# Attention with block summaries and an MLP on one core: summary scores of 128 queries, a spread on another engine, and a new order

## The chip, the cores and the metric

The kernel runs on one core of one Trainium2 chip. The metric is the device time of one launch in microseconds (us). Each launch is also seen by a profiler in one execution, whose span (first to last instruction) is somewhat shorter than its device time.

## What is computed

Inputs are q, k and v of shape (4, 8, 768, 64) in float32 (batch, heads, positions, channels) and the two weight matrices of an MLP, 512 x 2048 and 2048 x 512. Cut to what matters:

```
k_sum = k.reshape(B, H, 24, 32, D).max(axis=3)          # one summary key per 32 positions
v_sum = v.reshape(B, H, 24, 32, D).mean(axis=3)         # one summary value
scores_l = scale * q @ k^T, -1e9 where |i - j| >= 16    # near keys
scores_s = scale * q @ k_sum^T + log(32)                # 24 summary keys
a = softmax([scores_l, scores_s]) ;  x = a @ [v, v_sum] # (3072 tokens, 512)
h = x @ w_in ;  g = h * erf(softplus(h)) ;  out = g @ w_out
```

Of the near scores only those within 15 positions count, so a stretch of 64 queries needs a window of 96 keys, and with the 24 summaries 120 columns.

## The kernel before

The 3072 tokens are worked off in six chunks of 512. A **quad** is one chunk of one pair of heads (128 channels): 24 quads, four to a chunk. For a quad there are: the scores (`scores`, L479: near keys and summaries of eight blocks of 64 queries and two heads, into two banks of 4 x 120 columns), the softmax (`softmax`, L517: maximum on VectorE L535, exponential on ScalarE L541, reciprocal L553 on VectorE, normalization on VectorE L557 or ScalarE L560), eight transposes (`transp`, L571) and a copy on ScalarE (L575, tile `ptr`), the product with the values (`av`, L596, tile `px`) and a split of the result into a high and a low part (`xsplit`: `xh` is a cast on either engine, `xl` a subtraction on VectorE, L612). The MLP then runs in periods of four blocks of 128 columns: the first product (`mm1`, L635, tile `h`; each product is three matmuls, high by high, high by low and low by high), the activation, and the second product (`mm2`, L696 and L700, tile `ops`). Four quads make the 512 input channels of a chunk; so a chunk's first product needs all four quads, and quad p gives the p-th of its four parts.

Weights come as raw words (`rw`, loaded at L308, 1024 KB each) and are put together by VectorE in three steps (L325, L328, L331), then split into a high part (cast on ScalarE, L275) and a low part (VectorE, L347).

The first four quads have no earlier work to hide behind and take a way of their own. Their keys (`kf`, L420, 384 KB each), queries (`qf`, L421, 256 KB), the values of the sequence (`vt`, L425, two halves of 768 KB) and the windows of the values (`vwf`, L428, 384 KB) are loaded directly. VectorE reduces the summary keys (L431). TensorE sums the values into summaries (L437, six matmuls, tile `vs`), ScalarE copies them to `vsum` (L440), and they are spread into the last 24 rows of each quad's `vwf`: the first quad's by GpSimd (L443), the others' by a DMA each (L445, 96 KB). The scores are three steps: mask (L491, L492), near keys and summaries (both L500).

All that is written as operations with a duration for each engine that may do them, and `Plan.order` puts them in a row by list scheduling: the operation that can start first on an engine goes next; among those ready at that time, the one with the least key. The key is a due time (for TensorE the operation's number) plus an offset from the table `TUNE`, which has entries for the operations (1262 entries before, 1841 now). `FILL` puts matmuls with zeros ahead of chosen TensorE operations (`busy`, L738, tile `idle`); 14 more stand at the very start. Loads are issued by SP, in the planned order, on one queue.

The operations of the first quads that the change touches, as they are before:

```
on({"POOL": 1.1}, lambda e: e.tensor_copy(st[0]["vw"][LW:NK], vsum[LW:NK, 0:1, :].to_broadcast([NS, NB, 128])), ["vsum00"], ["vwg0"])
pe(0.5, lambda: keys(lambda r, j: [(LW, ksum[r, 0, qd])]), [f"qf{qd}", f"ksum0{qd}"], banks)
```

Of the kernel before, what the change touches and what calls it, by code (L numbers as in the profile page):

```python
# [26 lines left out]
NB = T // 64  # L27
NI = NB // 2
NT = T // 128
NS = 24  # L30
LW = 96
NK = LW + NS
# [12 lines left out]
FILL = {20: 7, 40: 8, 41: 9, 61: 6, 93: 14, 111: 6}  # L45
# [139 lines left out]
def block_attention_mlp(ctx: ExitStack, tc: tile.TileContext, q_t, k_nat, k_win, v_tok, v_nat, v_win, w_in, w_out, out):  # L185
    nc = tc.nc
# [7 lines left out]
    def sb(shape, dtype, name, tag=None):  # L194

        n = math.prod(shape[1:])
        if n % 128 == 0:
            return pool.tile(shape, dtype, name=name, tag=tag or name)
        t = pool.tile([128, -(-n // 128) * 128], dtype, name=name, tag=tag or name)[0:shape[0], 0:n]
        return t if len(shape) == 2 else t.rearrange("p (a b) -> p a b", a=shape[1]) if len(shape) == 3 else t.rearrange("p (a b c) -> p a b c", a=shape[1], b=shape[2])  # L200

    def ps(name, tag):
        return psum.tile([128, 2, 512] if tag == "pa" else [128, 512], F32, name=name, tag=tag)
# [48 lines left out]
    ksum = sb([128, 2, NP, NS], F32, "ksum")  # L252
    vrows = [slice(LW, NK), slice(0, NS)]
    vsum = sb([NK, NP, 128], F32, "vsum")
# [7 lines left out]
    def pe(us, fn, r=(), w=(), **kw):  # L262
        return P.add({"PE": us}, lambda e: fn(), r, w, **kw)

    def on(us, fn, r=(), w=(), **kw):
        return P.add(us, lambda e: fn(engines[e]), r, w, **kw)

    def act(us, fn, r=(), w=(), **kw):
        return P.add({"ACT": us}, lambda e: fn(), r, w, **kw)

    def dma(kb, fn, r=(), w=(), hold=2.0, **kw):
        return P.add({"SP": max(0.45, kb / 350.0)}, lambda e: fn(), r, w, hold=hold, **kw)
# [78 lines left out]
    def parts(m, n):  # L351
        u = ("o", m // 2, m % 2)
        split(u, n, f"a{m}", lambda: w32[u])
# [54 lines left out]
    st = {}  # L408
# [24 lines left out]
    def vsum_first(bank):  # L433
        def go(t):
            if t == 0:
                tiles[bank] = ps("vs", bank)
            nc.tensor.matmul(tiles[bank][0:NK], lhsT=pick[:, 20 - 4 * t:140 - 4 * t], rhs=vts[t // 3][:, t % 3], start=(t == 0), stop=(t == 5))  # L437
        for t in range(6):
            pe(0.87, lambda t=t: go(t), [f"vt{t // 3}"], [bank])
        act(0.5, lambda: nc.scalar.copy(vsum[LW:NK], tiles[bank][LW:NK].rearrange("s (p c) -> s p c", p=NP)), [bank], [f"vsum0{p}" for p in range(NP)])  # L440
        for p in range(NP):
            if p == 0:
                on({"POOL": 1.1}, lambda e: e.tensor_copy(st[0]["vw"][LW:NK], vsum[LW:NK, 0:1, :].to_broadcast([NS, NB, 128])), ["vsum00"], ["vwg0"])  # L443
            else:
                dma(100, lambda p=p: nc.sync.dma_start(out=st[p]["vw"][LW:NK], in_=vsum[LW:NK, p:p + 1, :].to_broadcast([NS, NB, 128])), [f"vsum0{p}"], [f"vwg{p}"])  # L445
# [33 lines left out]
    def scores(qd, banks=("pa",)):  # L479

        s = st[qd]

        def mask():
            for n in banks:
                tiles[n] = ps(n, n)
            s["sc"] = [tiles["pa"][:, 0], tiles["pa"][:, 1]] if banks == ("pa",) else [tiles[n] for n in banks]
            s["both"] = tiles["pa"] if banks == ("pa",) else None
            m0 = mask_at[qd // NP % 3]
            for sc in s["sc"] if qd < MQ else []:

                nc.tensor.matmul(sc[:, 0:NI * NK], lhsT=ident_h, rhs=mask_h[:, m0:m0 + NI], start=True, stop=False, skip_group_check=True)  # L491
                nc.tensor.matmul(sc[:, 0:NI * NK].rearrange("q (i c) -> q i c", i=NI)[:, :, LW:NK], lhsT=ones, rhs=cst.rearrange("o (i c) -> o i c", i=NI), start=False, stop=False, skip_group_check=True)  # L492

        def keys(parts):
            for j in range(NB):
                for a in range(2):
                    r, o = slice(64 * a, 64 * a + 64), slice(64 * (j % 2), 64 * (j % 2) + 64)
                    for n, rhs in parts(r, j):
                        n += j // 2 * NK
                        nc.tensor.matmul(s["sc"][a][o, n:n + rhs.shape[-1]], lhsT=s["qb"][r, 64 * j:64 * j + 64], rhs=rhs, start=qd >= MQ, stop=True, skip_group_check=True)  # L500

        def near(r, j):

            kn, k0 = kfirst[qd], 64 * j - 16
            return [(0, kn[r, k0:k0 + LW])] if j else [(0, kn[r, 0:16]), (16, kn[r, 0:LW - 16])]

        def both():
            mask()
            keys(lambda r, j: [(0, s["kw"][r, j])])
        if qd >= NP:  # L510
            pe(1.06 if qd >= MQ else 1.64, both, ["qb", "kw"] + (["mh"] if qd < MQ else []), banks)
        else:
            pe(0.58, mask, ["mh"], banks)
            pe(0.96, lambda: keys(near), [f"qf{qd}", f"kf{qd}"], banks)
            pe(0.5, lambda: keys(lambda r, j: [(LW, ksum[r, 0, qd])]), [f"qf{qd}", f"ksum0{qd}"], banks)
# [216 lines left out]
    banks = [("pa",), ("h0", "h1"), ("o0", "o1"), ("h0", "h1")]  # L732
    idle = ps("idle", "o3")

    def busy(n):

        for _ in range(n):
            nc.tensor.matmul(idle[:, 0:256], lhsT=zeros[:, 0:128], rhs=zeros, start=True, stop=True)  # L738
# [10 lines left out]
    for p in range(3):  # L749
        ksum_first(p)  # L750
        scores(p, banks[p])
        softmax(p, banks[p])
    vsum_first("o2")
    ksum_first(3)
    scores(3, banks[3])
    softmax(3, banks[3])
    convert(units[0])
# [31 lines left out]
    def attend(n):  # L789

        scores(n)
        softmax(n)
        load_quad_v(n)
# [95 lines left out]
    free = {"PE": 4.15, "DVE": 1.4, "ACT": 4.2, "POOL": 5.2, "SP": 0.7}  # L889
    plan = P.order(free, lambda n: 60 if n < 330 else 0, TUNE, "exp")  # L890
    sets = {"exp": "exp_and_others", "log": "natural_log_exp_and_others", "sig": "sigmoid_and_others"}
    filling = True
    for o in plan:
        if o["on"] == "PE":
            filling = filling and "o3" not in o["w"]
            if filling:
                busy(FILL.get(o["n"], 0))
        if "load" in o:
# [42 lines left out]
```

## Time and profile before

| | |
|---|---|
| runs | 636.8, 637.97, 638.75 us, median 637.97 |
| profiled execution | 638.24 us, span 635.3 us |
| TensorE busy | 629.0 us |
| ScalarE busy | 431.7 us |
| VectorE busy | 392.0 us |
| GpSimd busy | 19.6 us |
| moved by the DMA queues | 89.30 MB |

How it is read: busy time is the time in which an engine works on instructions; weight loads of TensorE (PEld) lie beside its matmuls. A chain of waits is followed back from the last instruction to what released each step. A table by stretches gives busy times and the busy share of the DMA engines between two times from the start of the span. A timeline lists an engine's instructions with start and duration, several of one kind in one row; instructions of a row overlap, so the duration of a row can reach past the start of the next.

### The profile page before, as it was taken

The numbers are of one execution on the slowest core, as the hardware profiler recorded it, in microseconds if no ns is written. First come the engines' busy times: TensorE is split into PE (matmuls) and PEld (weight loads), VectorE is DVE, ScalarE is ACT, GpSimd is POOL, SyncE is SP. The second block draws the span as 40 slices with busy tenths as digits, with TensorE's granted clock in tenths as the row PEclk, the third lists the DMA queues.
The fourth block names the chain that finished last, engine by engine and source line by source line (L and its number), as shares of the span: only waits on it lengthen the run. The fifth ranks groups of instructions, "written<-read, shape, count | busy, mean of one in ns | idle before, by whom it ended". The sixth has DMA issues, their size and how long they took to land.

```text
span 635.3 us, 10484 instructions
## 1 busy us (share of the span) xinstructions
PE 629.0 (99%) x4264; PEld 502.0 (79%) x4264; DVE 392.0 (62%) x502; ACT 431.7 (68%) x742; POOL 19.6 (3%) x56
## 2 busy tenths in 40 slices
PE   8999999999999999999999999999999999999997
PEld 6776557888888887888888888888888888888886
DVE  4999999756766647676655645735555454334442
ACT  5669977978949648976484684674954952863470
POOL 2001010100000000000000000000000000000000
PEclk9999999999999999999999999999999999999999
DMA  9998947724641334653152640224451103140013
GB/s 320 259 375 299 349 160 243 263 83 164 213 131 48 104 98 158 237 153 104 51 164 82 206 143 1 79 71 142 145 180 32 32 1 132 67 133 0 2 63 135
DMA packets 28483, 89.30 MB, mean 141 GB/s; under 512 B 3028, under 2 KB 8468, under 8 KB 23316
## 3 DMA queue, kind: packets, MB, share of 16 engines
q1 hardware_dynamic: 27860, 88.13, 41.9%
q8 instruction: 33, 0.54, 0.4%
q10 hardware_dynamic: 576, 0.52, 0.2%
q14 instruction: 14, 0.11, 0.1%
HBM read 75.89 MB, written 10.49 MB: 136 GB/s over the span
## 4 chain that ended last, share of the span: by engine, by line
PE 96%; DMA 2%; SPq 0%; ACT 0%; issue 0%; DVE 0%; ACTq 0%
PE h L635 41%; PE ops L700 38%; PE ops L696 4%; PE px L596 4%; PE pa L500 3%; PE pa L571 3%; DMA rw<-w_in 1%; PE vs L437 1%; DMA qf<-q_t 1%; PE idle L738 1%; PE vt L395 0%; SPq L445 0%; PE pa L491 0%; PE o L500 0%; PE h L500 0%
## 5 line engine op out<-in xcount | busy, mean ns | idle before, releaser
L635 PE MATMUL h<-xh,w 128*128 128x512 f32 x768 | 253.4, 396 | 0.0
L700 PE MATMUL ops<-w,gh 128*128 128x512 f32 x704 | 227.9, 393 | 0.0
L635 PEld LDWEIGHTS h<-xh,w 128*128 128x128 f32 x768 | 144.2, 188 | 32.1 <-issue 1.6
L700 PEld LDWEIGHTS ops<-w,gh 128*128 128x128 f32 x704 | 132.4, 188 | 28.4 <-issue 0.6
L635 PE MATMUL h<-xl,w 128*128 128x512 f32 x384 | 149.5, 389 | 0.0
L650 ACT ACTIVATE wt<-hc 128x1024 f32<-128x1024 f32 x48 | 50.7, 1057 | 136.5 <-DVE hc L275 136.4
L700 PE MATMUL ops<-w,gl 128*128 128x512 f32 x352 | 137.1, 390 | 0.0
L899 ACT ACT_TABLE_LOAD x105 | 134.7, 1283 | 1.9
L275 DVE COPY hc<-h 128x512 f32<-128x512 f32 x81 | 55.7, 690 | 124.0 <-PE h L635 123.4
L635 PEld LDWEIGHTS h<-xl,w 128*128 128x128 f32 x384 | 72.2, 188 | 15.1 <-issue 1.0
L700 PEld LDWEIGHTS ops<-w,gl 128*128 128x128 f32 x352 | 66.1, 188 | 13.0
L676 DVE TENSOR_TENSOR hc<-wt,hc 128x1024 f32<-128x1024 f32 x44 | 52.9, 1221 | 19.1 <-ACT wt L664 19.1
L659 ACT ACTIVATE wt<-wt,stats 128x1024 f32<-128x1024 f32 x48 | 55.4, 1153 | 0.6
L683 DVE TENSOR_TENSOR gl<-hc,gh 128x1024 fp32r<-128x1024 f32 x44 | 52.9, 1221 | 0.6
L541 ACT ACTIVATE pr<-pr,stats 128x120 f32<-128x120 f32 x128 | 48.7, 382 | 5.5 <-DVE stats L550 5.4
L664 ACT ACTIVATE wt<-wt 128x1024 f32<-128x1024 f32 x48 | 49.8, 1058 | 0.4
L275 DVE CAST gh<-hc 128x1024 fp32r<-128x1024 f32 x44 | 30.0, 692 | 28.0 <-PE ops L700 27.1
L575 ACT COPY ptr<-pa 120x1024 f32<-120x1024 f32 x24 | 24.2, 1009 | 12.0 <-PE px L596 6.5
L696 PE MATMUL ops<-a32s,gw 128*128 128x512 f32 x64 | 29.2, 595 | 0.0
L463 POOL COPY kw<-ksum 128x96 f32<-128x96 f32 (+1 forms) x28 | 14.8, 544 | 440.4 <-DMA kw<-k_win 440.4
L525 DVE TENSOR_TENSOR pr<-pa,mask_sb 128x960 f32<-128x960 f32 x16 | 18.5, 1157 | 10.3 <-PE pa L500 10.3
L596 PEld LDWEIGHTS px<-ptr,vw 120*64 120x64 f32 x640 | 20.3, 138 | 5.3 <-DVE hc L275 1.6
(110 smaller groups left out, 499.1 us busy)
## 6 DMA issues: line engine op xcount, KB each, us to landing
w<-dr SPq DMA_DIRECT2D x20, 1024.0 KB
kw<-k_win SPq DMA_DIRECT2D x20, 480.0 KB
rw<-w_in SPq DMA_DIRECT2D x8, 1024.0 KB
rw<-w_out SPq DMA_DIRECT2D x8, 1024.0 KB
vw<-v_win SPq DMA_DIRECT2D x20, 384.0 KB
qb<-q_t SPq DMA_DIRECT2D x20, 256.0 KB
rows<-k_nat SPq DMA_DIRECT2D x12, 384.0 KB
rows<-v_nat SPq DMA_DIRECT2D x12, 384.0 KB
```

The source lines that it names most:

```text
L275: e.copy(o, i) if e is nc.scalar else e.tensor_copy(o, i)
L541: nc.scalar.activation(s["pr"][:, j], s["pr"][:, j] if qd >= MQ else s["sc"][j // NI][:, i * NK:(i + 1) * NK], AF.Exp, scale=0.125, bias=s ...
L596: nc.tensor.matmul(xo[r, o], lhsT=s["vw"][:, j, r], rhs=s["pt"][:, a, o], start=True, stop=True)
L635: nc.tensor.matmul(hs[k, f][:, 0:T], lhsT=w[m], rhs=xt[ch, cc][x], start=(cc == 0 and n == 0), stop=(cc == 3 and n == 2))
L650: nc.scalar.activation(wt[k, s], hc[k, s], AF.Tanh, scale=0.5)
L659: act(1.06, lambda n=n: nc.scalar.activation(wt[k, n], wt[k, n], AF.Ln, scale=-0.49999994, bias=half_b), [s], [s], table=("log",))
L664: act(0.96, lambda n=n: nc.scalar.activation(wt[k, n], wt[k, n], AF.Erf, scale=-1.0), [s], [s], table=("sig",), after=after)
L676: e.tensor_tensor(hc[k, n], wt.pop((k, n)), hc[k, n], op=ALU.mult)
L683: e.tensor_tensor(gs[k, n][1], hc.pop((k, n)), f32(gs[k, n][0]), op=ALU.subtract)
L696: nc.tensor.matmul(os_[ch, t], lhsT=x[0][:, i % 2, t * 128:(t + 1) * 128], rhs=w32["o", g, i // 2][:, i % 2], start=first, stop=last)
L700: nc.tensor.matmul(os_[ch, t], lhsT=x[y][:, i % 2, t * 128:(t + 1) * 128], rhs=w[m], start=first and n == 0, stop=last and n == 2)
L899: nc.scalar.preload_act_table_set(sets[o["load"]])
```

## The change

Three parts. The summary scores of the first four quads are made for 128 queries and one head at a time, 8 matmuls a quad instead of 16 of 64 queries (a product of float32 runs as two records). The first quad's summary rows are spread by ScalarE instead of GpSimd. And both tables, `TUNE` and `FILL`, are new, so that the order on all engines, the first transfers' on SP among them, is another one. `FILL` has 57 matmuls with zeros instead of 50. From the new function on, line numbers are 7 higher.

```diff
-TUNE = {0: (-833.887, 1.5, 0, None), ...}
-FILL = {20: 7, 40: 8, 41: 9, 61: 6, 93: 14, 111: 6}
...
+FILL = {48: 5, 30: 9, 31: 4, 51: 7, 60: 8, 61: 4, 81: 5, 92: 15}
@@ vsum_first
             if p == 0:
-                on({"POOL": 1.1}, lambda e: e.tensor_copy(st[0]["vw"][LW:NK], vsum[LW:NK, 0:1, :].to_broadcast([NS, NB, 128])), ["vsum00"], ["vwg0"])
+                act(0.95, lambda: nc.scalar.copy(st[0]["vw"][LW:NK], vsum[LW:NK, 0:1, :].to_broadcast([NS, NB, 128])), ["vsum00"], ["vwg0"])
@@ scores
+        def summary():
+
+            for i in range(NI):
+                for a in range(2):
+                    r = slice(64 * a, 64 * a + 64)
+                    nc.tensor.matmul(s["sc"][a][:, i * NK + LW:i * NK + NK], lhsT=s["qb"][r, 128 * i:128 * i + 128], rhs=ksum[r, 0, qd], start=False, stop=True, skip_group_check=True)
+
...
-            pe(0.5, lambda: keys(lambda r, j: [(LW, ksum[r, 0, qd])]), [f"qf{qd}", f"ksum0{qd}"], banks)
+            pe(0.27, summary, [f"qf{qd}", f"ksum0{qd}"], banks)
```

The first place is SP's row of transfers between the first values and the fourth `vwf`. Before:

```order
L425 DMA vt<-v_tok 128x3x512 x2
L308 DMA rw<-w_in 128x2048
L428 DMA vwf<-v_win 96x1024
L421 DMA qf<-q_t 128x512
L428 DMA vwf<-v_win 96x1024
L308 DMA rw<-w_in 128x2048
L445 DMA vwf<-vsum 24x8x128 x2
L308 DMA rw<-w_in 128x2048
L428 DMA vwf<-v_win 96x1024
L445 DMA vwf<-vsum 24x8x128
L428 DMA vwf<-v_win 96x1024
```

And now, from the start on:

```order
L421 DMA qf<-q_t 128x512 x2
L420 DMA kf<-k_nat 128x768
L425 DMA vt<-v_tok 128x3x512
L420 DMA kf<-k_nat 128x768 x3
L421 DMA qf<-q_t 128x512
L425 DMA vt<-v_tok 128x3x512
L308 DMA rw<-w_in 128x2048
L428 DMA vwf<-v_win 96x1024
L421 DMA qf<-q_t 128x512
L428 DMA vwf<-v_win 96x1024
L308 DMA rw<-w_in 128x2048
L445 DMA vwf<-vsum 24x8x128 x3
```

Behind these stand a `w_in`, two `vwf` and a `w_in` now. Ahead of both pieces stand or stood the first keys and queries, of which two `kf` came first before and two `qf` and a `kf` now; the three transfers of `vsum` stand together, so the third is now ahead of the third `w_in` and the third `vwf`.

The second place is TensorE from the third quad's product with its values (`px`) to the end of the fourth's. Before:

```order
L596 MATMUL px<-ptr,vwf 64x64 x16
L635 MATMUL h<-xh,w 128x512
L635 MATMUL h<-xl,w 128x512
L635 MATMUL h<-xh,w 128x512
L571 MATMUL pa<-ident,prf 120x128 x8
...
L635 MATMUL h<-xh,w 128x512
L596 MATMUL px<-ptr,vwf 64x64 x16
L635 MATMUL h<-xh,w 128x512
L635 MATMUL h<-xl,w 128x512
...
L738 MATMUL idle<-zeros 128x256
```

And now:

```order
L603 MATMUL px<-ptr,vwf 64x64 x16
L578 MATMUL pa<-ident,prf 120x128 x8
L642 MATMUL h<-xh,w 128x512
L642 MATMUL h<-xl,w 128x512
...
L642 MATMUL h<-xh,w 128x512
L603 MATMUL px<-ptr,vwf 64x64 x16
L642 MATMUL h<-xh,w 128x512
L642 MATMUL h<-xl,w 128x512
```

The fourth quad's transposes (`pa`) stood three matmuls of the first product behind the third `px` and nine ahead of the fourth; they now stand directly behind the third `px`, with nine between them and the fourth. The six matmuls with zeros behind the fourth are gone. Ahead of the third `px`, the same happened to the third transposes: they stood ahead of the second `px`, with 18 matmuls of the first product between it and the third, and stand behind it now, with three such matmuls ahead of the second `px` and 15 between.

The third place is VectorE from the first quad's split on. Before:

```order
L275 CAST xh<-px 128x512
L550 TENSOR_SCALAR stats<-stats 128x8
L612 TENSOR_TENSOR xl<-px,xh 128x512
L325 TENSOR_SCALAR a_489<-rw 128x1024
L328 SCALAR_TENSOR_TENSOR a_489<-rw,a_489 128x1024
L331 SCALAR_TENSOR_TENSOR a_489<-rw,a_489 128x1024
L612 TENSOR_TENSOR xl<-px,xh 128x512
L545 TENSOR_SCALAR stats<-stats 128x8
L325 TENSOR_SCALAR a_538<-rw 128x1024
L553 RECIPROCAL stats<-stats 128x8
L328 SCALAR_TENSOR_TENSOR a_538<-rw,a_538 128x1024
L347 TENSOR_TENSOR w<-a_489,w 128x1024
```

And now:

```order
L557 TENSOR_SCALAR stats<-stats 128x8
L619 TENSOR_TENSOR xl<-px,xh 128x512
L325 TENSOR_SCALAR a_439<-rw 128x1024
L328 SCALAR_TENSOR_TENSOR a_439<-rw,a_439 128x1024
L331 SCALAR_TENSOR_TENSOR a_439<-rw,a_439 128x1024
L552 TENSOR_SCALAR stats<-stats 128x8
L560 RECIPROCAL stats<-stats 128x8
L619 TENSOR_TENSOR xl<-px,xh 128x512
L325 TENSOR_SCALAR a_526<-rw 128x1024
L328 SCALAR_TENSOR_TENSOR a_526<-rw,a_526 128x1024
L331 SCALAR_TENSOR_TENSOR a_526<-rw,a_526 128x1024
L347 TENSOR_TENSOR w<-a_439,w 128x1024
```

The cast `xh` of the first quad went to ScalarE; the fourth quad's reciprocal went ahead of the second `xl` and of the third weight's first step (L325); the second weight's last step (L347) went behind the third weight's first three.

## Rows read from the trace of the kernel before

**Rows 1.** The page: busy time of each engine, and the chain by engine.

```profile
PE 629.0 (99%) x4264; PEld 502.0 (79%) x4264; DVE 392.0 (62%) x502; ACT 431.7 (68%) x742; POOL 19.6 (3%) x56
...
PE 96%; DMA 2%; SPq 0%; ACT 0%; issue 0%; DVE 0%; ACTq 0%
```

**Rows 2.** The table by stretches: busy us of each engine, clock, DMA share, GB/s.

```profile
core 0: us, PE busy (x) PEld busy (x) DVE busy (x) ACT busy (x) POOL busy (x), PEclk, DMA share, GB/s
6.90:16.20 9.30, 8.55 (x234) 6.80 (x235) 6.04 (x13) 5.59 (x32) 0.00 (x0) 1.00 1.05 396
16.20:34.10 17.90, 17.53 (x207) 12.84 (x206) 16.73 (x25) 12.62 (x43) 1.11 (x1) 1.00 1.00 259
42.20:80.00 37.80, 37.80 (x196) 23.84 (x194) 37.35 (x44) 36.21 (x54) 1.81 (x2) 1.00 0.92 336
34.10:631.70 597.60, 597.60 (x3800) 479.18 (x3800) 366.64 (x460) 409.80 (x664) 14.80 (x28) 1.00 0.40 132
```

**Rows 3.** Groups by line: busy us, mean ns of one, idle before.

```profile
L738 PE MATMUL idle<-zeros 128*128 128x256 bf16 x64 | 9.7, 305 | 1.1 <-DVE zeros L210 1.1
...
L500 PE MATMUL h<-ksum,qf 64*64 64x24 f32 x64 | 1.3, 210 | 0.0
L443 POOL COPY vwf<-vsum 24x1024 f32<-24x1024 f32 x1 | 1.1, 1107 | 15.8 <-ACT vsum L440 15.8
```

**Rows 4.** Timeline of SP: start us, duration us, transfers that it issues.

```profile
9.10 0.33 SPq L308 DMA_DIRECT2D rw<-w_in  x1
21.34 1.82 SPq L445 DMA_DIRECT2D vwf<-vsum  x2
...
23.79 0.43 SPq L428 DMA_DIRECT2D vwf<-v_win  x1
```

**Rows 5.** Timeline of TensorE, 7 to 43 us.

```profile
7.68 0.67 PE L500 MATMUL h<-ksum,qf 64*64 64x24 f32 x32
8.28 0.94 PE L738 MATMUL idle<-zeros 128*128 128x256 bf16 x7
...
28.32 1.15 PE L596 MATMUL px<-ptr,vwf 120*64 120x64 f32 x32
...
34.07 1.15 PE L596 MATMUL px<-ptr,vwf 120*64 120x64 f32 x32 [0.27 <-ACT prf L560]
...
35.97 1.04 PE L571 MATMUL pa<-ident,prf 128*120 128x128 f32 x8
36.76 0.47 PE L635 MATMUL h<-xh,w 128*128 128x512 f32 x1
...
38.69 0.40 PE L635 MATMUL h<-xh,w 128*128 128x512 f32 x1
39.02 1.15 PE L596 MATMUL px<-ptr,vwf 120*64 120x64 f32 x32
...
41.60 0.83 PE L738 MATMUL idle<-zeros 128*128 128x256 bf16 x6
42.19 0.47 PE L635 MATMUL h<-xh,w 128*128 128x512 f32 x1
```

**Rows 6.** Timelines of ScalarE and VectorE, 20 to 33 us.

```profile
20.73 0.58 ACT L440 COPY vsum<-vs 24x512 f32<-24x512 f32 x1 [0.48 <-PE vs L437]
21.66 1.01 ACT L575 COPY ptr<-pa 120x1024 f32<-120x1024 f32 x1 [0.35 <-PE pa L571]
...
30.78 1.07 ACT L575 COPY ptr<-pa 120x1024 f32<-120x1024 f32 x1
...
26.82 0.68 DVE L275 CAST xh<-px 128x512 fp32r<-128x512 f32 x1
...
27.53 0.69 DVE L612 TENSOR_TENSOR xl<-px,xh 128x512 fp32r<-128x512 f32 x1
...
32.27 0.69 DVE L325 TENSOR_SCALAR a<-rw 128x1024 uint32<-128x1024 uint32 x1 [0.25 <-DMA rw<-w_in]
```

**Rows 7.** The chain of waits of 20 to 36 us: start us, us, what.

```profile
23.21 9.04 DMA rw<-w_in
```

2 lines of the change are left out of this document (1 added, 1 removed).

## The prediction

> **What bounds the kernel now.** I read the page's busy shares and its chain of waits first. TensorE is busy 629.0 of 635.3 us and holds 96% of the chain [rows 1], so only work that leaves TensorE, or time in which it does nothing useful, can shorten the run. The table by stretches says where such time can be: from 34.1 us to 631.7 us TensorE is busy in every microsecond, 597.6 us in all; before 34.1 it is not [rows 2]. The group of idle matmuls (L738) shows that even the early busy time is partly filler: 64 of them, 9.7 us [rows 3]. The diff touches no instruction of the dense stretch except its order. It can win in one place, the start up to about 42 us, where TensorE's fillers and gaps lie: the dense stretch loses no matmul, all of the first and the second product are in both orders. It can lose anywhere, if the new order makes TensorE wait.
>
> What bounds the start is the transfers. The 16 DMA engines have a busy share of 1.05 from 6.9 to 16.2 us and of 1.00 from there to 34.1 [rows 2]. SP issues nothing between 9.10 and 21.34 us, since it waits for vsum [rows 4], and the engines stay full: they work off a queue. The first matmuls that the dense stretch cannot do without are those of the third quad's product with its values (L596, px): they begin at 34.07, after 0.27 us of idle [rows 5]. The profile puts that idle down to ScalarE's L560, which px does not read. What it reads are ptr (its third copy begins at 30.78 and takes 1.07 us, so it was there by 31.85 [rows 6]) and vwf. The third vwf was issued at 23.79 [rows 4], directly behind the third w_in transfer, which was issued at 23.21 and took 9.04 us to land, at 32.25 [rows 7]. So I read the wait at 34.07 as that for the vwf transfer, and call its end X: 34.07 in the run before.
>
> **The change part by part.** Summary scores: 64 summary matmuls of 64 queries become 32 of 128. Before, a quad's 16 (32 records) run from 7.68 to the filler at 8.28, 0.60 us; four quads 2.4 us [rows 3, 5]. No row has a matmul with 64 rows and 128 columns of weights on a 24-column stream. Bounds for a quad: 0.30 us, half the count at the same spacing, and 0.60, no gain; I take 0.3 (fewer loads of weights, each wider), so 1.2 us of TensorE work go. All of it lies before X, with 50 of the 64 fillers issued among and behind it, so it is worth nothing unless X comes earlier. If that cover were gone it would be worth its 1.2 us.
>
> Spreading the first summary rows: GpSimd's copy takes 1.11 us [rows 3]; on ScalarE I take 1.0, like the ptr copy of the same 1024 columns [rows 6], bounds 0.6 (vsum's 512 columns) and 1.1. The first px waits for it in either case. ScalarE's queue behind it holds the first weight cast, which waits for VectorE. Worth nothing on the path; at worst 1.0 us before X, again covered.
>
> ScalarE also copies ptr (1.01 us) ahead of vsum now; before, vsum's copy began at 20.73 [rows 6]. SP's three vsum transfers wait for it, and the third w_in and both vwf transfers are queued behind them. The first scores need 896 KB to have come instead of 1024 (two q and a k ahead of and with their own, not two k and a q), at 259 to 396 GB/s [rows 2] 0.3 to 0.5 us earlier, so I expect vsum between 20.2 and 21.7, a microsecond either way of before.
>
> First transfers: the bytes ahead of the third vwf are the same ones in another order (four k, four q, two halves of v, three w_in, two vwf, two vsum: 8128 KB) plus the third vsum transfer, 96 KB, which stood behind it and now stands in front. At 259 GB/s [rows 2] 96 KB are 0.38 us. Ends: 0, if it fits a gap between other transfers; and 0.9, the time that SP takes to issue one (two in 1.82, [rows 4]). I take 0.4, since the engines and not SP were the full ones: X goes from 34.07 to 34.5. A later issue of the w_in transfer costs nothing as long as the queue is full until then, which the share of 1.00 says it is.
>
> Here a rule of the Trainium skill speaks against the move: "DMA: Bandwidth & Descriptors", section "Why a DMA increments its semaphore by 16 and not by 1", says that a transfer is split over the largest number of engines up to 16 that divides its slowest dimension. With 24 rows that would be 12 engines; an estimate by that page is 0.38 x 16/12 = 0.5 us, and X would be 34.6 instead of 34.5. No row here shows single engines.
>
> Is TensorE ready at X? The second px begins at 28.32, behind xl of the first quad, which ends at 28.22 on VectorE and was preceded there by the cast xh (26.82) [rows 5, 6]. In the new order ScalarE does that cast, so VectorE reaches xl up to 0.7 us earlier (27.53 less 26.82); but three matmuls of L642 stand ahead of the second px now, two of them behind xl (0.5): the second px at 28.1 to 28.8. Behind it stand px itself 1.15, the third transposes 0.79 (35.97 to 36.76) and 15 matmuls of L635 at 0.24 (eight of them from 36.76 to 38.69), 3.6, together 5.55 us [rows 5]: the third px could start at 33.65 to 34.35. It would then sit idle for 0.15 to 0.85 us until X. The early gains end in that wait.
>
> From X on: before, X to 42.19 is 8.12 us, of which the filler from 41.60 to 42.19 is 0.59 and a gap before the last px (38.69 + 0.24 to 39.02) 0.09 [rows 5]. The new order has no filler there; the fourth transposes now stand directly behind the third px, so ScalarE's ptr copy runs beside nine L635 matmuls (2.2 us against 1.0 plus latencies) and the last px finds it done. Both go: 0.7 us. Ends: 0, if the last quad's xl comes as late as before, and 0.7.
>
> VectorE: before, the reciprocal of the fourth quad stood behind the weight step L325, which waited 0.25 us for w_in until 32.27 [rows 6]; now it stands ahead. That frees ScalarE's normalization by some 2 us, but what is late next is again vwf, so it is worth nothing by itself. Dense stretch: VectorE is busy 37.35 of 37.80 us from 42.2 to 80 [rows 2], TensorE all of it. With the same instructions there I take 0, bounds 0 to 2.8 us lost (below), none won, since a full engine cannot be fuller.
>
> Sum, against the profiled execution: 635.3 + 0.4 - 0.7 = 635.0 us of span. That execution took 638.24, 2.94 around its span; so 637.9. The median of the three runs is 637.97, 0.27 lower, so I forecast **637.7**.
>
> **The rivals.**
> A, the third vwf is not what X waits for, or it lands earlier. For it: the profile names another releaser, and bytes of other rows may pass. Then X is TensorE's own 33.65: 0.4 won, and 0.7 behind it: 634.2 of span, 637.1, or **636.9** on the median. If the second px comes earlier by the summary's 1.2 us as well, 635.7. Against it: the DMA shares and the order of the queue.
>
> B, slower: VectorE starves TensorE in the dense stretch. Place: the third weight's step L325 and what follows. In the new order VectorE does the second weight's last step not while the third is in transfer but behind it, and two reductions of k rows and one more h copy come later too: four instructions, at the length of L325, 0.69 us [rows 6], 2.8 us of work by which the weights may be behind, with no filler left on TensorE to take that up. It decides from the point where this is more than what the new order puts off on TensorE too (the scores of quad 4 move back behind two more groups of 12 matmuls of L635). If all 2.8 us come through: 637.8 of span, **640.5**. Against it: the loads of those k rows are put later together with their readers.
>
> C, the queue runs dry: vsum's copy comes over 1.5 us later, the w_in transfer is issued after the queue is empty, and X moves by 1.5 us more: 636.5 of span, **639.2**.
>
> D, the summary matmuls cost as much as before (0.6 a quad): the start of the second px above doesn't count on the saving, so this gives the forecast's time, no other.
>
> **How the numbers follow.** The forecast (with D) has 0.50, from 636.9 to 639.0 by its bounds (X 34.07 to 35.0, gain 0 to 0.7: 637.3 to 638.9, and a little for the runs, which lie between 636.8 and 638.75). A 0.30, B 0.12, C 0.08. About 0.3%, 1.9 us, is what a measurement of this kernel can tell from no change: faster means under 636.06, slower over 639.88. Of A half is under 636.06, where the second px comes earlier too, and a little of the forecast: 0.20. B gives most of slower, C a little: 0.12. The rest, 0.68, is within. The range leaves out the far end of A and most of B: 635.6 to 639.5.
>
> **What would show it.** In the new profile: the third px (now L603) starting at 34 to 35 us, behind an idle of some tenths of a microsecond, with TensorE's last L642 before it ending at 33.6 to 34.3: then the transfers bound the start. A start at 33.7 or earlier without idle is A. Three vsum issues in a row from about 21.5, the w_in issue at 24. The summary group (L512) at half the records and under 2.6 us busy. No filler and no gap behind X. TensorE full in every stretch from 36 us; if waits for VectorE or for weights show up between 40 and 110 us, it is B. I am wrong if the time before X shrinks with the matmuls taken from it, or if the dense stretch is shorter than 597.6 us.

## The result: a little slower

The changed kernel took 638.91 us in the median of 22 runs, the kernel before 637.39 in 22 runs beside it; the ratio is 1.0032, with a 95% interval from 1.0019 to 1.0044. The time lies inside the range, but the change is a loss of some 1.5 to 2 us where 0.3 us of gain was forecast, and the mechanism of the forecast is not the one that sets the time.

The profiled execution has a span of 636.2 us, 0.9 over that of before; it is the shortest of the 22, whose median span is 637.1, so the traces compared here show less than the whole loss. First the page (busy us and share of each engine; the chain by engine), against [rows 1]:

```profile
PE 631.4 (99%) x4207; PEld 504.3 (79%) x4207; DVE 391.6 (62%) x501; ACT 431.9 (68%) x743; POOL 16.7 (3%) x55
...
PE 99%; DVE 0%; ACT 0%; issue 0%
```

With fewer matmuls in the summaries TensorE is busy for 2.4 us more, and no transfer is in the chain any more. The table by stretches (busy us of each engine, clock, DMA share, GB/s), against [rows 2]:

```profile
6.90:16.20 9.30, 9.24 (x136) 6.28 (x134) 6.72 (x12) 4.94 (x29) 0.00 (x0) 1.00 1.04 391
16.20:34.10 17.90, 17.90 (x217) 14.28 (x216) 15.48 (x25) 13.89 (x48) 0.00 (x0) 1.00 0.85 246
```

TensorE has almost no gap left ahead of 34.1 us (0.06 us up to 16.2, none behind), and the DMA engines, full before, are at 0.85 from 16.2 to 34.1 us. The timeline of TensorE from the first scores to the end of the start (start us, duration us, instructions), against [rows 5] and, first, the first scores of before:

```profile
6.94 0.97 PE L500 MATMUL h<-kf,qf 64*64 64x16 f32 x36 [0.53 <-DMA qf<-q_t]
```

```profile
5.99 0.97 PE L500 MATMUL o<-kf,qf 64*64 64x16 f32 x36
6.90 1.07 PE L512 MATMUL o<-ksum,qf 64*128 64x24 f32 x16
7.91 0.72 PE L745 MATMUL idle<-zeros 128*128 128x256 bf16 x5
...
27.65 1.80 PE L745 MATMUL idle<-zeros 128*128 128x256 bf16 x15
29.20 0.47 PE L642 MATMUL h<-xh,w 128*128 128x512 f32 x1
...
30.07 1.15 PE L603 MATMUL px<-ptr,vwf 120*64 120x64 f32 x32
...
35.61 1.15 PE L603 MATMUL px<-ptr,vwf 120*64 120x64 f32 x32
...
39.80 1.15 PE L603 MATMUL px<-ptr,vwf 120*64 120x64 f32 x32
...
42.86 0.62 PE L642 MATMUL h<-xh,w 128*128 128x512 f32 x2
```

Three things are to be seen. A quad's new summaries (L512) run from 6.90 to the filler at 7.91, 1.01 us, where the 32 records of before took 0.60 [rows 5]. The second px starts at 30.07 instead of 28.32, behind fifteen fillers, which hold TensorE until 29.20, and three matmuls of the first product; from the first keys to it TensorE needs 24.08 us instead of 21.38. And the third px starts at 35.61 with no idle ahead of it: X is 1.54 us later, and it is TensorE's own. Behind it 0.64 us come back: the 37th matmul of the first product, which stood at 42.19 before, is the second of the pair that begins at 42.86, at 43.09, so the way from X takes 7.48 us instead of 8.12. The sum is 0.90, and that is all: from the 37th matmul to the end of the span both executions take 593.1 us.

### The profile page after: what moved, and what is told of

It reads as the page before. It is cut to its first block, busy times and chain, and to the rows that moved or that the text cites. A ratio compares the mean times of both kernels' runs of the same rounds, so it can differ in the third digit from the quotient of the medians.

```text
span 636.2 us, 10373 instructions
## 1 busy us (share of the span) xinstructions
PE 631.4 (99%) x4207; PEld 504.3 (79%) x4207; DVE 391.6 (62%) x501; ACT 431.9 (68%) x743; POOL 16.7 (3%) x55
## 4 chain that ended last, share of the span: by engine, by line
PE 99%; DVE 0%; ACT 0%; issue 0%
PE h L642 42%; PE ops L707 38%; PE ops L703 4%; PE px L603 4%; PE pa L578 3%; PE pa L500 3%; PE idle L745 2%; PE vs L437 1%; PE vt L395 0%; PE pa L491 0%; PE h L512 0%; PE h L500 0%; PE h L491 0%; PE pa L512 0%; PE o L512 0%; PE o L500 0%
## 5 line engine op out<-in xcount | busy, mean ns | idle before, releaser
L552 DVE TENSOR_SCALAR stats<-stats 128x8 f32<-128x8 f32 x24 | 4.1, 169 | 40.0 <-ACT pr L548 39.6
L463 POOL COPY kw<-ksum 128x96 f32<-128x96 f32 (+1 forms) x28 | 13.0, 479 | 459.2 <-DMA kw<-k_win 388.5
```

## The experiments

T is the theory that TensorE is the bound of the new start, C that the transfers are. The ratios are to the kernel before, run beside each; the spans are medians of all executions. The spans tell the kernels apart better than the times, since the time around the span is 1.7 to 3.1 us in executions of the kernel before and 1.7 to 1.9 in most of the changed ones, which no run here explains. No spans of before stand beside the first 22 runs. Eight of the fourteen intervals include 1.0000: by their times these kernels don't differ from the kernel before beyond noise, and what is said of the size of their effects rests on medians of 11 or 12 spans and on the traces.

| label | ratio, 95% interval | median span, before's beside it |
|---|---|---|
| a_sum64 | 1.0005 (0.9988 to 1.0022) | 636.1, 635.7 |
| a_fill3 | 1.0004 (0.9990 to 1.0019) | 636.3, 635.7 |
| b_sum128 | 1.0008 (0.9995 to 1.0022) | 637.0, 635.7 |
| b_act | 0.9989 (0.9976 to 1.0002) | 634.9, 635.7 |
| a_sum64_fill3 | 1.0011 (0.9988 to 1.0034) | 636.2, 635.3 |
| a_order | 1.0025 (1.0006 to 1.0045) | 637.0, 635.3 |
| b_sum128h | 1.0051 (1.0031 to 1.0071) | 639.5, 635.3 |
| b_act_pool | 1.0011 (0.9997 to 1.0025) | 636.0, 635.3 |
| after_again | 1.0032 (1.0018 to 1.0046) | 638.6, 635.8 |
| a_vsum | 1.0035 (1.0014 to 1.0057) | 638.0, 635.8 |
| b_act2 | 0.9993 (0.9978 to 1.0008) | 635.0, 635.8 |
| b_best | 1.0023 (1.0003 to 1.0043) | 637.5, 635.8 |
| a_kwact | 1.0021 (1.0007 to 1.0036) | 637.5, 635.8 |
| a_good | 0.9989 (0.9977 to 1.0002) | 635.2, 635.8 |

**The summaries: a_sum64, b_sum128, b_sum128h.** In the kernel after they are undone, in the kernel before they are added alone, and once more with one head behind the other.

```diff
a_sum64 (after)
-            pe(0.27, summary, [f"qf{qd}", f"ksum0{qd}"], banks)
+            pe(0.27, lambda: keys(lambda r, j: [(LW, ksum[r, 0, qd])]), [f"qf{qd}", f"ksum0{qd}"], banks)
b_sum128 (before), with summary() as in the change
-            pe(0.5, lambda: keys(lambda r, j: [(LW, ksum[r, 0, qd])]), [f"qf{qd}", f"ksum0{qd}"], banks)
+            pe(0.5, summary, [f"qf{qd}", f"ksum0{qd}"], banks)
b_sum128h (b_sum128)
-            for i in range(NI):
-                for a in range(2):
+            for a in range(2):
+                for i in range(NI):
```

> The kernel after, with its summary scores made by 16 matmuls of 64 queries a quad again; order and fillers stay. Theory T (TensorE is the bound of the start: it runs without a gap from 5.99 us to the third px at 35.61, and the summaries of 128 queries take 1.0 us a quad instead of 0.6): the third px starts 1.2 to 1.6 us earlier, at 34.0 to 34.4, and the time falls by 1.2 to 1.6 us, from about 1.5 over the kernel before to about level with it. Theory C (the late vsum transfers and the w_in transfer behind them set the third px): the third px stays at 35.6 behind an idle of over a microsecond, and the time stays 1.5 us over before.

> The kernel before with the new summary scores alone; the order and the fillers are those of before. Theory T: 0.4 us more TensorE work for each of four quads, of which two stand ahead of the wait of 0.71 us before the third's summaries and so are taken up by it; the other two, 0.8 us, less the wait of 0.27 at the third px: 0.5 us slower than before, at most 1.6. Theory C, and the forecast's own (D at worst): no change, within 0.3 us.

> The kernel before with summaries of 128 queries, all four of one head first and then those of the other, instead of the heads in turn. If matmuls of the two heads overlap each other when they come in turn, a quad's 16 records now take longer than 1.0 us and the time rises over that of the version in turn (637.0 of span). If what counts is the weights of 128 columns that each of them loads, it stays 1.0 us a quad and the time as it was, 1.1 to 1.3 us over before.

Undoing them brings the median span from 637.1, that of the first 22 runs, to 636.1, adding them to the kernel before brings it from 635.7 to 637.0 (the measured times differ by less, 1.0008). In the profile of a_sum64 the second px comes 0.95 us earlier, but the third doesn't: it now waits (TensorE's timeline).

```profile
29.12 1.15 PE L603 MATMUL px<-ptr,vwf 120*64 120x64 f32 x32
...
35.91 1.15 PE L603 MATMUL px<-ptr,vwf 120*64 120x64 f32 x32 [1.18 <-ACT w L275]
```

So in this execution the third px is where C has it, and the median span where T has it. The wait isn't always there: of five profiles with the new tables and the old summaries two have it (1.06 us in a_vsum), and in a_sum64_fill3, a_order and a_good the third px starts without one, at 34.28, 34.71 and 34.80. T holds for the kernel after, and C stands close behind it.

The profile of b_sum128 says less than its median. Its third px starts at 34.06, as in before, since the first keys came 0.85 us earlier; from these keys to the third px it needs 27.97 us instead of 27.13. That its span is 1.5 over before's has another reason, a wait near 179 us. TensorE's row in the table of waits (us in all, times, longest us) and VectorE's timeline:

```profile
PE pa L578 <- DVE pr L564: 1.4, 1, 1.4
```

```profile
175.79 0.95 DVE L388 TENSOR_REDUCE vs_sum<-rows 128x24 f32<-128x768 f32 x1 [3.50 <-DMA rows<-v_nat]
```

VectorE waits for a transfer of values and comes late with a normalization. Five of the seven profiles with the old tables have this wait (0.17 to 1.48 us; before and b_act2 don't), none of the nine with the new tables has it. So 1.3 us is no clean price of the summaries, and b_sum128h has 1.48 us of that wait as well. What the summaries themselves take is read from their rows, and the order of the heads tells what they cost. TensorE's timelines of b_sum128 and of b_sum128h:

```profile
7.00 1.08 PE L512 MATMUL h<-ksum,qf 64*128 64x24 f32 x16
8.01 0.94 PE L745 MATMUL idle<-zeros 128*128 128x256 bf16 x7
```

```profile
8.31 1.54 PE L512 MATMUL h<-ksum,qf 64*128 64x24 f32 x16
9.79 0.94 PE L745 MATMUL idle<-zeros 128*128 128x256 bf16 x7
```

Sixteen records take 1.01 us with the heads in turn and 1.48 with one behind the other, and the 32 of 64 x 64 took 0.60: 63, 92 and 19 ns a record. Wider loads of weights (187 ns each instead of 134) can't be all of it, since they are the same in both orders: matmuls of the two heads, which lie on different parts of the array, overlap. With blocks of 64 rows and 64 columns four parts take turns, with 64 rows and 128 columns two, and with one head at a time one. This is what "TensorEngine Tiling (Array Packing)", sections "Available Configurations" and "Key Properties", of the Trainium skill says (four tiles of 64 x 64, two of 64 x 128, which load weights and multiply independently of each other); the three rows agree in their order. In proportion they don't: two parts in turn are 1.5 times as fast as one, four parts, with narrower blocks, 4.8 times. And a head is both a half of the rows and a bank of scores of its own, so the runs don't tell which of the two lets the heads overlap.

**The fillers: a_fill3, a_sum64_fill3.**

```diff
a_fill3 (after); a_sum64_fill3 has the edit of a_sum64 as well
-FILL = {48: 5, 30: 9, 31: 4, 51: 7, 60: 8, 61: 4, 81: 5, 92: 15}
+FILL = {48: 5, 30: 9, 31: 4, 51: 7, 60: 8, 61: 4, 81: 5, 92: 3}
```

> The kernel after with 3 instead of 15 matmuls with zeros ahead of its first matmuls of the first product. Theory T: those begin about 1.0 us earlier (at 28.2, behind xl, which ends at 28.15, instead of 29.20), the third px at 34.6, the time 1.0 us less than after, 0.5 over before. Theory C: the gap goes into an idle before the third px; no change of the time. A third possibility: without them TensorE's clock falls, and the time rises by a microsecond or more.

> The kernel after with both undone: 16 summary matmuls of 64 queries a quad, and 3 instead of 15 zeros ahead of the first product. Each alone brought the span down by 0.8 to 1.0 us (medians of the spans: 637.1 after, 636.1 and 636.3). If TensorE alone is the bound of the start, both add up: median span about 635.3, 0.4 under before (635.7). If the transfers are right behind it (with the old summaries alone the third px waited 1.18 us), the second gain goes into that wait: about 636.1, as with the old summaries alone.

Twelve fillers less are worth 0.8 us of median span with the new summaries, against the first 22 runs, and nothing with the old ones (636.1 and 636.2, on two chips, beside 635.7 and 635.3). The expectation has the gain go into a wait in that case, but the profiled execution of a_sum64_fill3 doesn't show one: its third px starts at 34.28 without a wait, and its span is 635.0. Three of its twelve executions had a mean clock of 0.997. So where the gain goes in the median isn't shown. The profiled execution of a_fill3 shows the gain only beside its first wait: TensorE waited 1.23 us for its first keys (0.05 in the kernel after), and yet the second px starts at 30.14, 0.07 later than in the kernel after, and the third at 35.67.

**ScalarE's spread: b_act, b_act2, b_act_pool.** The first in the kernel before alone, twice; the third with the other three spreads taken from the DMA queue to GpSimd.

```diff
b_act, b_act2 (before)
-                on({"POOL": 1.1}, lambda e: e.tensor_copy(st[0]["vw"][LW:NK], vsum[...]), ...)
+                on({"POOL": 1.1}, lambda e: nc.scalar.copy(st[0]["vw"][LW:NK], vsum[...]), ...)
b_act_pool (b_act)
-                dma(100, lambda p=p: nc.sync.dma_start(out=st[p]["vw"][LW:NK], in_=vsum[...]), ...)
+                dma(100, lambda p=p: nc.gpsimd.tensor_copy(st[p]["vw"][LW:NK], vsum[...]), ...)
```

> The kernel before with the first summary rows spread by ScalarE instead of GpSimd, at the same place in the order. Both theories: no change, within 0.3 us of before, since it lies beside TensorE's scores and fillers. If it delays ScalarE's first weight cast so that the first product waits, up to 1.0 us slower.

> The kernel before with ScalarE's spread, once more. If GpSimd's copy held VectorE up (in before L331 takes 1.94 us beside it, 1.23 without), the second px comes 0.6 to 0.7 us earlier, and the median span is 0.4 to 0.8 us under before, as in its first 12 runs (634.9 against 635.7). If that was chance: no difference.

> The kernel before with the first spread by ScalarE and the other three by GpSimd (three copies) instead of DMAs, at the same places in the order: SP no longer waits for vsum, the third w_in and vwf transfers are issued some 10 us earlier. If the third px is bound by these transfers (theory C for the kernel before), it starts without an idle at 33.3 to 33.8, and the span is 0.5 to 1.0 us less than with ScalarE's spread alone (634.9), 1.3 to 1.8 less than before. If not, it is as with that alone, 634.9.

I had expected nothing of b_act, and its median span is 0.8 us under before's, twice. Something that was overlooked stands in the timelines of GpSimd and VectorE of the kernel before:

```profile
21.38 1.11 POOL L443 COPY vwf<-vsum 24x1024 f32<-24x1024 f32 x1 [15.78 <-ACT vsum L440]
```

```profile
21.62 1.94 DVE L331 SCALAR_TENSOR_TENSOR a<-rw,a 128x1024 uint32<-128x1024 uint32 x1
```

and in that of VectorE of b_act:

```profile
21.15 1.23 DVE L331 SCALAR_TENSOR_TENSOR a<-rw,a 128x1024 uint32<-128x1024 uint32 x1
```

A step of 1.23 us takes 1.94 beside GpSimd's copy, and VectorE's row behind it, with the first quad's xl, is late by that. Other profiles with such a copy show it too (1.94 in b_sum128; in a_order a step of 1.16 us takes 1.85).

That the 0.8 us come from it isn't shown. The second px starts at 27.69 and 27.65 in the two profiles, 28.32 before, but TensorE is 0.46 us earlier there already at the first transposes, ahead of GpSimd's copy (20.07 and 20.08; 20.54 before), which leaves 0.2 for the shorter step. And the third px waits in both, 2.04 and 0.57 us, and starts at 35.19 and 33.71, so the gain ahead of it doesn't reach it.

With three copies on GpSimd it is two steps that are held up, in b_act_pool (GpSimd, then VectorE):

```profile
20.60 5.19 POOL L445 COPY vwf<-vsum 24x1024 f32<-24x1024 f32 x3 [14.98 <-ACT vsum L440]
```

```profile
21.04 1.94 DVE L331 SCALAR_TENSOR_TENSOR a<-rw,a 128x1024 uint32<-128x1024 uint32 x1
22.90 1.99 DVE L557 TENSOR_TENSOR prf<-prf,stats 128x960 f32<-128x960 f32 x1
```

Here it is on the path: the second px starts at 28.74, behind a wait of 1.34 us for xl, and what the earlier transfers win is lost; the third px needs no wait, but starts at 34.12. "SBUF — State Buffer", section "SBUF: two separate sides", of the Trainium skill has the rule: VectorE and GpSimd share a pair of ports, which an instruction of VectorE with two inputs from SBUF, or one of GpSimd that reads SBUF, holds for its whole length while the other stands still. The rows agree: L331 and L557 have two inputs, and the copy reads vsum.

**The order: a_order, a_vsum, b_best.** The first is the kernel after with the old summaries and GpSimd's spread; the second is a_sum64_fill3 with ScalarE's copy of vsum ahead of the first ptr copy; the third is b_act with two operations moved.

```diff
a_order (a_sum64)
-                act(0.95, lambda: nc.scalar.copy(st[0]["vw"][LW:NK], vsum[...]), ...)
+                on({"ACT": 0.95}, lambda e: nc.gpsimd.tensor_copy(st[0]["vw"][LW:NK], vsum[...]), ...)
a_vsum (a_sum64_fill3), behind plan = P.order(...)
+    ahead(vcopy, ptr)
b_best (b_act), behind plan = P.order(...)
+    ahead(first(w=["vwf2"]), first(w=["w2"]))
+    ahead(recip, step)
```

> The kernel after with the old summary matmuls and with GpSimd for the first spread, each at the same place in the order: order, fillers and first transfers alone. By the parts measured so far (all three together 1.4 us of span, the summaries 1.0 to 1.3, ScalarE's spread -0.8 in the order of before) they would cost 0.9 to 1.2 us over before. If the spread by ScalarE is worth nothing in the new order, 0.1 to 0.4 us over before.

> The kernel after with old summaries and 3 zeros (a_sum64_fill3), and with the copy of vsum put ahead of the first ptr copy on ScalarE, as in before; nothing else. If what is left over before (about 0.5 to 0.9 us of median span) comes from SP issuing the third w_in and vwf 2.5 us later, the copy now begins at 21.4 instead of 22.4, these transfers come a microsecond earlier, and the span falls by up to 0.9 us, to about before's. If it comes from elsewhere in the order, no change, or up to 1 us more, since the first px waits for ptr.

> The kernel before with ScalarE's spread, with the third vwf transfer issued ahead of the third w_in transfer, and with the fourth quad's reciprocal ahead of the weight step that waits for that w_in. If the third px waits for its vwf transfer (it did by 2.04 us in the profile with ScalarE's spread alone), it now starts behind TensorE's own work, at 33.0 to 33.6 us, without an idle; the w_in transfer lands up to 1.5 us later, and VectorE's third weight with it. Span 0.5 to 1.2 us under that with ScalarE's spread alone. If the later w_in holds up VectorE's xl and the last px as much, no gain.

a_order is 1.7 us of median span over before (1.0025), more than either case of its expectation, with neither of the other two parts in it, so the tables alone lose time. Its profiled execution doesn't show where: it is the shortest of the twelve, with before's span (635.3). a_vsum doesn't mend the loss (638.0). SP issues the third w_in at 23.45 there, 2.4 us earlier than in a_sum64_fill3, and yet the third px starts at 35.23, behind a wait of 1.06 us, so the late issue alone isn't what is left; its profile has the wait near 72 us that comes next, too. b_best does what it should at the third px (33.28, no wait), but VectorE now waits for w_in, and the fourth quad's part of the first product for VectorE:

```profile
33.88 0.69 DVE L325 TENSOR_SCALAR a<-rw 128x1024 uint32<-128x1024 uint32 x1 [2.60 <-DMA rw<-w_in]
```

```profile
33.28 1.15 PE L596 MATMUL px<-ptr,vwf 120*64 120x64 f32 x32
...
38.76 0.50 PE L635 MATMUL h<-xl,w 128*128 128x512 f32 x1 [1.64 <-DVE xl L612]
```

The last case of its expectation: no gain, a loss of 1.7 us of median span. Five of its twelve executions had a mean clock of 0.996 or 0.997; the median of the others is 636.0. That the third px has no wait once its vwf goes ahead of the w_in bears out how the prediction read the wait of before.

**The wait near 72 us: after_again, a_kwact, a_good.** after_again is the kernel after; in a_kwact one copy of the sixth quad goes from GpSimd to ScalarE; a_good has the old summaries and 3 fillers as well.

```diff
a_kwact (after), a_good (a_sum64_fill3)
-            on({"POOL": 0.1 + 0.05 * n}, lambda e, b=b, js=js, n=n: e.tensor_copy(s["kw"][:, js, LW:NK], ksum[...]),
+            on({"POOL": 0.1 + 0.05 * n}, lambda e, b=b, js=js, n=n: copy(nc.scalar if qd == 5 else e, s["kw"][:, js, LW:NK], ksum[...]),
```

> The kernel after once more, beside the others on one chip. Its median span is 1.2 to 1.6 us over before, as in the first 22 runs. In the profile: TensorE without a wait between the first keys and the third px; where the first keys land later than at 5.99 us, the third px moves by as much, since nothing in between takes it up.

> The kernel after with the sixth quad's copy of summary keys (L463, two instructions) made by ScalarE instead of GpSimd, at the same place in the order; all else as it is. If VectorE's two-input steps hold GpSimd's copy up and that is what the order costs: no wait of 1.9 us near 72 us in any profile, and the median span falls by 0.5 to 1.7 us from after's 637.1 and 638.6, to about 636.6 to 637, with nothing between 638 and 640 except at a lower clock. If the cost lies elsewhere: 637 to 638.6 as before.

> The same, with the old summary matmuls and 3 instead of 15 zeros as well. If summaries, fillers and GpSimd's copy are what the change costs, the median span is at or below before's (635.3 to 635.8), as ScalarE's first spread, which is worth 0.7, is still in it: 634.8 to 635.8. If the order has another cost, it stays at 636.2 or above.

The median span of after_again is 2.8 us over before's instead of 1.2 to 1.6. Its profile fell on a long execution, 643.4 us of span. Its timelines of GpSimd, VectorE and TensorE:

```profile
71.22 5.79 POOL L463 COPY kw<-ksum 128x96 f32<-128x96 f32 x2 [18.17 <-DMA kw<-k_win]
```

```profile
70.91 2.35 DVE L328 SCALAR_TENSOR_TENSOR a32s<-rw,a32s 128x1024 uint32<-128x1024 uint32 x2
73.18 2.35 DVE L331 SCALAR_TENSOR_TENSOR a32s<-rw,a32s 128x1024 uint32<-128x1024 uint32 x2
75.45 1.22 DVE L678 TENSOR_TENSOR gw<-wt,hc 128x1024 f32<-128x1024 f32 x1
```

```profile
76.85 1.05 PE L500 MATMUL pa<-kw,qb 64*64 64x120 f32 x32 [1.95 <-POOL kw L463]
```

The first profile of the kernel after has the same three places, but GpSimd came first:

```profile
66.01 0.90 POOL L463 COPY kw<-ksum 128x96 f32<-128x96 f32 x2 [16.60 <-PE pa L578]
```

```profile
67.35 2.35 DVE L328 SCALAR_TENSOR_TENSOR a32s<-rw,a32s 128x1024 uint32<-128x1024 uint32 x2
69.61 2.36 DVE L331 SCALAR_TENSOR_TENSOR a32s<-rw,a32s 128x1024 uint32<-128x1024 uint32 x2
```

The new order puts five steps of two inputs in a row on VectorE, directly behind the time at which the sixth quad's keys land: two L328, two L331 and L678. If GpSimd's copy begins ahead of them, it takes 0.9 us; if the keys come a little later, it is through 0.3 us behind the last of the five (77.01 and 76.67), after 5.8 us, and TensorE waits for 1.95. Of seven profiles with the new tables and this copy on GpSimd three show that wait (1.94 to 1.96 us): in these the copy begins 0.1 to 0.3 us behind the first of the five steps, in the other four 0.8 to 1.4 us ahead of it.

With the copy on ScalarE the wait is gone from the profile, and so are the executions between 638 and 640 us at a full clock, of which after_again had seven in 13, the first 22 runs three, and a_kwact none in 11. That these are the ones with the wait is read from the profiled executions: with it 638.1 and 638.8 us (and 643.4 at a lower clock), without it 635.0 to 636.4. The median span falls from 638.6 to 637.5 beside the same 635.8 of before, not to the 636.6 to 637 expected, and the two ratios don't differ beyond noise. What is left in a_kwact are the summaries and the fillers: without them a_good is at 635.2, 2.3 us less and 0.6 under before, as expected, though its interval includes 1.0000.

## Why the prediction was wrong, point by point

**The summaries** are the step that failed most. Bounds of 0.30 and 0.60 us a quad were taken from the spacing of the records of 64 x 64, as if a record cost the same whatever part of the array it fills, and "no gain" was the upper end. It measured 1.01, some 1.6 us more for four quads instead of 1.2 less. The loss of the change starts here. Rival D, which had the same time as the forecast, should have been a price above 0.60.

**"Is TensorE ready at X?"** failed by two steps. The start of the second px was taken from VectorE's xl (28.1 to 28.8); it was 30.07, since TensorE itself was late: the sum began at VectorE and left out TensorE's own way from the first keys, 24.08 us. And the fillers were counted as cover. They are instructions in a row like any other and don't shrink: xl began at 27.46 and took 0.69 us, so it was there by 28.15, but the first matmul of the first product stood behind fifteen fillers until 29.20. The way from the second px to the third was right: 5.54 us measured, 5.55 by the sum.

**X** was forecast at 34.5, set by the transfers, and was 35.61, set by TensorE. The vsum copy came at 22.46, later than the 20.2 to 21.7 expected, as it stands behind ScalarE's exponentials and ptr copy now; SP issued the three vsum transfers from 23.07 and the w_in at 25.76:

```profile
22.46 0.58 ACT L440 COPY vsum<-vs 24x512 f32<-24x512 f32 x1
```

```profile
23.07 2.64 SPq L445 DMA_DIRECT2D vwf<-vsum  x3
25.76 0.54 SPq L308 DMA_DIRECT2D rw<-w_in  x1
```

So the queue did run dry, as in rival C (share 0.85), but that set the time only where TensorE's work had been cut (the wait of 1.18 us in a_sum64). C's time, 639.2, is near the measured one for another reason.

**From X on**: right. 0.7 us forecast, 0.64 measured, and no filler and no gap stand there.

**ScalarE's spread**, "worth nothing on the path", was probably wrong to the good: a median span 0.8 us shorter in two experiments, neither clear of noise, and how it comes about stays open. What the sum left out is that GpSimd's copy holds VectorE up by 0.7 us; the row that told it, L331 at 1.94 us beside other such steps at 1.22, was in the trace of before and was not asked why.

**The dense stretch** at 0 was right for the profiled execution (593.1 us from the 37th matmul on, in both) and not for all others. Its bound, 0 to 2.8 us lost, holds the 1.9 us that are lost in some of them, and rival B named VectorE's weight steps; but its mechanism, weights that come late, is not what happens. VectorE is in time there and keeps GpSimd from its copy.

Together, in median spans: new summaries 1.0 to 1.3 (the latter with the wait near 179 us in it), fillers up to 0.8, the wait near 72 us 1.1 in one set, ScalarE's spread -0.8. They don't add up exactly: the transfers stand close behind TensorE at X, and most of them are not clear of noise one by one. Clear is what they make together, 638.6 in after_again and 635.2 in a_good.

## What to carry to other kernels

Ask how many parts of TensorE's array take turns before matmuls are merged: half the instructions on twice the columns can take longer. A filler ahead of useful work is cover only as long as the engine would wait anyway, and is a cost from the moment another change makes it late. A step that takes longer in one place than its twins elsewhere is the row to explain first; here it showed that VectorE's two-input steps and GpSimd's copies should not stand beside each other. And a longer execution is the edit's doing only as far as the trace shows it at the edit's place: in b_sum128 a wait near 179 us made up 1.44 of 1.5 us.

## What the runs showed of the hardware

GpSimd's copy of 0.9 us took 5.8 beside five steps of VectorE in a row, without getting in between them, and which of the two came first hung on when the keys' transfer landed, so one order of instructions gave two times, 1.9 us apart.

A wait can be followed by a lower clock, and then costs more than its length. In after_again the first keys came late and TensorE stood still for 1.38 us up to 8.21; from about 10 to 13 us the granted clock was 0.50, the level of 1.2 GHz, and again lower behind the wait of 1.95 us (the table by stretches; the columns are those of [rows 2]):

```profile
10.00:11.00 1.00, 1.00 (x8) 0.77 (x9) 0.56 (x1) 0.00 (x0) 0.00 (x0) 0.50 1.04 403
77.00:80.00 3.00, 3.00 (x38) 2.37 (x35) 2.03 (x4) 2.97 (x3) 0.00 (x1) 0.68 0.85 344
```

The first keys came 2.22 us later than in the first profile of the kernel after, the third px 3.56, so the stretch between them took 1.34 us more. In a_sum64 a wait of 1.96 us at the place of the second was followed by a clock of 1.00, and so was one of 1.57 us for the first keys in b_sum128h. What decides between the two is left open, as is how much of the changed kernel's long executions (four of its first 22 had a mean clock of 0.997 and spans of 640.8 us and more) is due to it.
